# Linear attention and an MLP on one core: even and odd partition runs, weight loads held back, and transposes moved from TensorE to DMA

## The chip, the cores and the metric

The kernel runs on one core of a Trainium2 chip. The metric is device time in microseconds (us) of one execution. The profile is one profiled execution; its span runs from the first to the last instruction and is about 1.7 us shorter than the time of the same run.

Names: PE is TensorE's matmuls, PEld its weight loads, DVE is VectorE, ACT is ScalarE, POOL is GpSimd, SP is SyncE, whose queue issues most transfers here. k(0) is the k input of batch 0, and so on.

## The reference

There are 8 batches of 8 heads, 576 tokens and 64 values per head. Attention is linear, with features of relu times a cosine and a sine of the token's position; then a token-wise MLP follows.

```python
def phi(x, c, s):
    r = np.maximum(x, 0.0)
    return np.concatenate([r * c, r * s], axis=-1)      # 64 -> 128 features
q_p = phi(q, cos_w, sin_w)
k_p = phi(k, cos_w, sin_w)
kv = np.einsum('bhsf,bhsd->bhfd', k_p, v)
z = np.sum(k_p, axis=2)
num = np.einsum('bhsf,bhfd->bhsd', q_p, kv)
den = np.einsum('bhsf,bhf->bhs', q_p, z)[..., None] + 1e-06
x = num / den                                           # then: tokens x 512
h = x @ w_in                                            # 512 x 2048
g = h * np.cos(h)
out = g @ w_out                                         # 2048 x 512
```

## The kernel before

For each batch the 576 tokens lie as 4 tiles of 128 tokens and a remainder of 64, which two batches share. So one half of the 128 partitions holds five tokens each and the other half four. `half(n)` says which half: 64 consecutive partitions. Every load of k, v or q is two transfers, one to each half.

```python
    def half(n):
        return slice(R * n, R * (n + 1))            # R = 64
    ...
    def load(b, name, after=None):
        ...
        if after is not None:                       # holds the load back until `after` is there
            for hf in range(2):
                nc.gpsimd.tensor_copy(
                    out=m[R * hf:R * hf + 1, 0, 0, 0:1], in_=after)
        s_ = srcs[name][b]
        nc.sync.dma_start(
            out=m[half(n)], in_=s_[:, 0:S5, :].rearrange("h (p t) d -> p h t d", t=NT + 1))
        nc.sync.dma_start(
            out=m[half(1 - n), :, 0:NT, :],
            in_=s_[:, S5:S, :].rearrange("h (p t) d -> p h t d", t=NT))
```

The matmuls of this kernel take q features and x with the contracted dimension on the partitions. TensorE transposes both itself, and ACT copies the result out of PSUM, the memory that its matmuls write (`x_trans` is the same with four matmuls a tile):

```python
    def q_trans(b, t):
        ...
        for h in range(H):
            nc.tensor.matmul(
                QP[:, h, :], lhsT=src[:, h].rearrange("p g d -> p (g d)"),
                rhs=IDENT, is_transpose=True)
        qT = apool.tile([P, H, P], F16, name=f"qT{b}_{t}", tag=f"qT{t}")
        nc.scalar.activation(out=qT, in_=QP, func=AF.Copy)
```

The weights are loaded by POOL's queue in four transfers each, cast from f32 to f16 on the way (the page counts 4.19 MB on that queue for the two matrices, which are 8.39 MB in f32). A one-element copy from a tile that a load fills holds a transfer back, because the transfer overwrites that element: POOL's copy for w_out waits 18.24 us for v(1), until 45.65 us, and its transfer leaves at 46.12. Only the first of four is held:

```python
    for name in ("k", "v", "q"):
        load(0, name)
    ...
    nc.gpsimd.tensor_copy(out=w_in_sb[0:1, 0, 0:1], in_=raw[("v", 0)][0:1, 0, 0, 0:1])
    for g in range(4):
        fs = slice(g * Dff // 4, (g + 1) * Dff // 4)
        nc.gpsimd.dma_start(out=w_in_sb[:, :, fs], in_=wi[:, :, fs])
    for f in attention(0, after=w_in_sb[0:1, 0, Dff // 2:Dff // 2 + 1]):
        f()
    nc.gpsimd.tensor_copy(out=w_out_sb[0:1, 0, 0:1], in_=raw[("v", 1)][0:1, 0, 0, 0:1])
    # ... w_out in four transfers
    for s in range(B + 1):                          # MLP of batch s beside attention of batch s+1
        spread(mlp(s), attention(s + 1) if s + 1 < B else [])
```

A scheduler in the build orders each engine's instructions, so the order on an engine need not be that of the code. The traces show it.

## Time and profile before

| | before |
|---|---|
| median of 3 runs | 353.27 us (353.17 to 353.39) |
| span of the profiled run | 351.6 us |
| PE busy, matmuls | 305.9 us, 2448 |
| first matmul of batch 1's MLP | 74.42 us |
| last matmul ends | 345.8 us |

From the profile's page of the kernel before, parts 1 and 2. The rows of part 2 cut the span into 40 slices; a digit is the busy share in tenths.

```profile
PE 305.9 (87%) x2448; PEld 170.8 (49%) x2448; DVE 202.8 (58%) x491; ACT 185.4 (53%) x284; POOL 13.3 (4%) x30
...
PE   0034477799999999999999999999999999999993
...
DMA  7999999829998578940993168202021020220232
```

There are two regimes. From slice 9 to the last but one TensorE is always busy. Before it, TensorE idles much of the time and the DMA row stands mostly at 9. The view of busy time by stretch, asked for the second regime, with the columns named in its header:

```profile
core 0: us, PE busy (x) PEld busy (x) DVE busy (x) ACT busy (x) POOL busy (x), PEclk, DMA share, GB/s
74.42:345.80 271.38, 270.13 (x2109) 148.47 (x2107) 164.54 (x388) 150.19 (x233) 0.00 (x0) 1.00 0.46 99
```

TensorE is idle for 1.25 us of 271.38, at full clock (1.00). Here a matmul removed is time removed. The list of TensorE's waits, longest first (tile, source line, releaser: total, times, longest), lies almost wholly in the first regime:

```profile
PE KV_0_136 L129 <- DVE V_0_75 L118: 17.3, 1, 17.3
PE XP_0_304 L183 <- DVE x_0_254 L174: 5.5, 1, 5.5
PE QP_0_184 L142 <- ACT qp_111 L98: 5.5, 1, 5.5
PE M_362 L237 <- DMA w_in_sb<-in_moe_w_in_dram: 3.0, 1, 3.0
PE QP_0_462 L142 <- DVE qp_352 L100: 2.5, 1, 2.5
PE KV_0_398 L129 <- DVE V_1_76 L118: 1.8, 1, 1.8
```

Why the inputs come late is on POOL's timeline (start, duration, instruction):

```profile
6.44 2.36 POOL L334 DMA_DIRECT2D w_in_sb<-in_moe_w_in_dram  x3
...
45.65 0.18 POOL L337 CAST w_out_sb<-vm_131 1x1 f16<-1x1 f32 x1 [18.24 <-DMA vm_131<-in_v_dram]
```

Weight transfers that nothing holds back leave from 6.44 us and share the DMA engines with k, v and q of batch 0. v(1), which the last line waits for, lands at 45.65 us.

What a transpose costs is on TensorE's timeline between back-to-back matmuls:

```profile
102.64 0.81 PE L237 MATMUL M_1134<-xT_354,w_in_sb 128*128 128x512 f16 x3
103.28 0.39 PE L183 MATMUL XP_1_1142<-IDENT,x_1_1062 128*128 128x128 f16 x4
103.51 1.06 PE L249 MATMUL M_1149<-xTr_717,w_in_sb 128*128 128x128 f16 x16
```

Durations overlap in the pipeline (102.64 + 0.81 is past 103.28), so the cost is start to start: the four x transposes hold TensorE from 103.28 to 103.51, about 0.225 us. Eight q transposes hold it 0.445 us by the same reading (120.83 to 121.27 for one group).

### The profile page before, as it was taken

How to read it: one execution, taken by the hardware profiler on the slowest of the kernel's cores; microseconds unless marked ns; L12 is line 12 of the kernel's file. 1: busy time of each engine (PE TensorE's matmuls, PEld its weight loads, DVE VectorE, ACT ScalarE, POOL GpSimd, SP SyncE). 2: the span in 40 equal slices, each digit the busy share in tenths (PEclk: the TensorE clock that was granted, in tenths of full speed). 3: DMA queues.
4: the chain of work that ended last, by engine and by line, in shares of the span. 5: the costliest groups of instructions: out<-in, count | busy, mean ns of one | idle time of the engine just before them, and what ended most of it. 6: DMA issues, size and time to landing. Idle time of an engine off the chain costs nothing.

```text
span 351.6 us, 6070 instructions
## 1 busy us (share of the span) xinstructions
PE 305.9 (87%) x2448; PEld 170.8 (49%) x2448; DVE 202.8 (58%) x491; ACT 185.4 (53%) x284; POOL 13.3 (4%) x30
## 2 busy tenths in 40 slices
PE   0034477799999999999999999999999999999993
PEld 0034235445565555445574554455655554446441
DVE  0421849989996669438784887445943471444100
ACT  1335437665755575356764665557555753555210
POOL 9120010000000000000000000000000000000000
PEclk9998589989999999999999999999999999999999
DMA  7999999829998578940993168202021020220232
GB/s 152 224 235 248 250 200 237 149 58 209 202 203 170 135 163 158 204 122 10 238 196 85 34 132 184 72 2 62 1 47 44 2 62 0 60 49 13 68 83 60
DMA packets 33083, 42.37 MB, mean 121 GB/s; under 512 B 1824, under 2 KB 30496, under 8 KB 33056
## 3 DMA queue, kind: packets, MB, share of 16 engines
q1 hardware_dynamic: 28544, 37.75, 50.3%
q0 software_dynamic: 4224, 4.19, 7.1%
q8 instruction: 19, 0.31, 0.4%
q10 hardware_dynamic: 288, 0.04, 0.1%
q14 instruction: 8, 0.07, 0.1%
HBM read 36.74 MB, written 9.44 MB: 131 GB/s over the span
## 4 chain that ended last, share of the span: by engine, by line
PE 79%; DMA 5%; issue 5%; DVE 4%; ACT 2%; POOL 1%; POOLq 0%
DMA w_in_sb<-in_moe_w_in_dram 5%; ACT ch L229 1%; PE M_4128 L261 1%; PE M_4109 L261 1%; PE M_4049 L261 1%; PE M_2824 L261 1%; PE M_2741 L261 1%; PE M_2601 L261 1%; PE M_2250 L261 1%; PE M_1948 L261 1%; PE M_1815 L261 1%; PE M_1732 L261 1%; PE M_1592 L261 1%; PE M_1454 L261 1%; PE M_1241 L261 1%
## 5 line engine op out<-in xcount | busy, mean ns | idle before, releaser
L237 PEld LDWEIGHTS <-w_in_sb 128*128 128x128 f16 x512 | 47.2, 99 | 48.6 <-issue 7.6
L129 PE MATMUL KV_0_136<-V_0_75,kp_110 128*128 128x65 f16 x16 | 1.2, 243 | 17.3 <-DVE V_0_75 L118 17.3
L249 PEld LDWEIGHTS <-w_in_sb 128*128 128x128 f16 x256 | 14.8, 98 | 0.2
L129 PEld LDWEIGHTS <-kp_110 128*128 128x128 f16 x32 | 2.2, 131 | 17.3 <-issue 17.3
L261 PEld LDWEIGHTS <-g_3761 128*128 128x128 f16 x64 | 6.2, 97 | 7.6
L261 PEld LDWEIGHTS <-g_3287 128*128 128x128 f16 x64 | 6.2, 98 | 7.3
L261 PEld LDWEIGHTS <-g_751 128*128 128x128 f16 x64 | 6.2, 98 | 7.1
L261 PEld LDWEIGHTS <-g_1760 128*128 128x128 f16 x64 | 6.2, 98 | 7.1
L261 PEld LDWEIGHTS <-g_2769 128*128 128x128 f16 x64 | 6.2, 98 | 7.1
L261 PEld LDWEIGHTS <-g_2278 128*128 128x128 f16 x64 | 6.1, 98 | 7.1
L261 PEld LDWEIGHTS <-g_1269 128*128 128x128 f16 x64 | 6.1, 98 | 7.1
L261 PEld LDWEIGHTS <-g_361 128*128 128x128 f16 x64 | 6.1, 98 | 7.1
L142 PEld LDWEIGHTS <-qp_111 128*128 128x128 f16 x32 | 3.3, 148 | 5.6 <-ACT qp_111 L98 5.6
L142 PE MATMUL QP_0_184<-IDENT,qp_111 128*128 128x128 f16 x8 | 1.0, 311 | 5.5 <-ACT qp_111 L98 5.5
L183 PE MATMUL XP_0_304<-IDENT,x_0_254 128*128 128x128 f16 x4 | 0.7, 301 | 5.5 <-DVE x_0_254 L174 5.5
L100 DVE TENSOR_SCALAR KPR_78<-km_124,CS 64x512 f16<-64x512 f32 x2 | 0.9, 487 | 7.8 <-DMA km_124<-in_k_dram 7.8
L98 ACT ACT_TABLE_LOAD x1 | 1.3, 1283 | 7.2 <-DMA km_83<-in_k_dram 7.2
L100 DVE TENSOR_SCALAR qp_1753<-qm_1483,CS 128x512 f16<-128x512 f32 x8 | 3.7, 461 | 1.9 <-PE QP_3_1486 L142 1.9
L230 DVE TENSOR_TENSOR g_3761<-M_3762,ch 128x512 f16<-128x512 f32 x1 | 0.7, 692 | 6.9 <-ACT ch L229 6.9
L237 PE MATMUL M_362<-xT_113,w_in_sb 128*128 128x512 f16 x4 | 1.9, 622 | 3.0 <-DMA w_in_sb<-in_moe_w_in_dram 3.0
L100 DVE TENSOR_SCALAR qp_2762<-qm_2492,CS 128x512 f16<-128x512 f32 x8 | 3.7, 461 | 1.3 <-PE QP_3_2495 L142 1.3
L98 ACT ACTIVATE qp_111<-qm_89,CS 128x512 f16<-128x512 f32 x4 | 2.6, 711 | 3.1 <-DMA qm_89<-in_q_dram 3.1
(1128 smaller groups left out, 864.6 us busy)
## 6 DMA issues: line engine op xcount, KB each, us to landing
out_dram<-ost SPq DMA_DIRECT2D x32, 256.0 KB, 3.2
w_in_sb<-in_moe_w_in_dram POOLq DMA_DIRECT2D x4, 512.0 KB, 16.8
w_out_sb<-in_moe_w_out_dram POOLq DMA_DIRECT2D x4, 512.0 KB, 17.5
out_dram<-ostr SPq DMA_DIRECT2D x8, 128.0 KB, 2.3
km_83<-in_k_dram SPq DMA_DIRECT2D x1, 640.0 KB, 6.4
vm_86<-in_v_dram SPq DMA_DIRECT2D x1, 640.0 KB, 10.7
qm_89<-in_q_dram SPq DMA_DIRECT2D x1, 640.0 KB, 16.6
km_124<-in_k_dram SPq DMA_DIRECT2D x1, 640.0 KB, 10.5
```

What stands on the lines that cost most here:

```text
L98: nc.scalar.activation(out=out[:, :, g, :], in_=in_, func=AF.Relu, scale=sc)
L100: nc.vector.tensor_scalar(out=out[:, :, g, :], in0=in_, scalar1=0.0, scalar2=sc, op0=ALU.max, op1=ALU.mult)
L129: nc.tensor.matmul(KV[:, hh, :], lhsT=kp[:, t, h].rearrange("p g d -> p (g d)"), rhs=V1[b % 2][:, t, h, :], start=(t == 0), stop=False)
L142: nc.tensor.matmul(QP[:, h, :], lhsT=src[:, h].rearrange("p g d -> p (g d)"), rhs=IDENT, is_transpose=True)
L183: nc.tensor.matmul(XP[:, c, :], lhsT=x2[:, c * P:(c + 1) * P], rhs=IDENT, is_transpose=True)
L229: nc.scalar.activation(out=ch[:, 0:n], in_=M1, func=AF.Sin, bias=PIH, scale=1.0)
L230: nc.vector.tensor_tensor(out=dst, in0=M1, in1=ch[:, 0:n], op=ALU.mult)
L237: nc.tensor.matmul(M1, lhsT=w_in_sb[:, c, j * P:(j + 1) * P], rhs=xts[b][:, c, :], start=(c == 0), stop=(c == NCT - 1))
L249: nc.tensor.matmul(M1[:, jj, :], lhsT=w_in_sb[:, c, j * P:(j + 1) * P], rhs=xts[("r", pr)][:, c, :], start=(c == 0), stop=(c == NCT - 1))
L261: nc.tensor.matmul(M2, lhsT=gts[key][:, j, gsl], rhs=w_out_sb[:, j, :], start=(j == 0), stop=(j == NJT - 1))
```

## The change

It has three intents. The two runs of partitions become the even and the odd ones, so that each load and store spreads over the whole range of partitions. All four transfers of w_in wait for the first of q(0)'s two transfers, all four of w_out for v(1), and q is loaded before v. From batch 2 on, q features and x are transposed by DMA from and to the on-chip memory, not by TensorE and ACT. Beside these, the remainder becomes a fifth tile, padded with zeros, and V is cast in one instruction of five tiles. The core of the diff, cuts marked:

```diff
+    NPE = 2
-    def half(n):
-        return slice(R * n, R * (n + 1))
+    def blocks(ap, n):
+        return ap.rearrange("(p f) ... -> f p ...", f=2)[n]
 ...
-        nc.sync.dma_start(
-            out=m[half(n)], in_=s_[:, 0:S5, :].rearrange("h (p t) d -> p h t d", t=NT + 1))
-        nc.sync.dma_start(
-            out=m[half(1 - n), :, 0:NT, :],
-            in_=s_[:, S5:S, :].rearrange("h (p t) d -> p h t d", t=NT))
 ...
+        nc.sync.dma_start(out=blocks(m, n), in_=five)
+        nc.sync.dma_start(out=blocks(m, 1 - n)[:, :, 0:NT, :], in_=four)
 ...
     def prep_v(b):
 ...
-        nc.vector.tensor_copy(
-            out=V1[b % 2][:, :, :, 0:D],
-            in_=m[:, :, 0:NT, :].rearrange("p h t d -> p t h d"))
-        nc.vector.tensor_copy(out=V1R[b % 2][hf, :, 0:D], in_=m[hf, :, NT, :])
+        vt = raw["v"].rearrange("p h t d -> p t h d")
+        for n, (t0, t1) in enumerate(((0, 2), (2, NT + 1)) if b == 0 else ((0, NT + 1),)):
+            dst = V1[b % 2][:, t0:t1, :, 0:D]
+            if b == 0 and n == 0:
+                nc.scalar.activation(out=dst, in_=vt[:, t0:t1], func=AF.Copy)
+            else:
+                nc.vector.tensor_copy(out=dst, in_=vt[:, t0:t1])
 ...
+    def q_trans_dma(b):
+        qT = apool.tile([P, NT + 1, H, P], F16, name=f"qT{b}", tag="qTd")
+        nc.sync.dma_start_transpose(
+            out=qT.rearrange("f t h p -> f (t h) p"),
+            in_=qps[b].rearrange("p t h g d -> p (t h g d)"))
 ...
     def x_trans(b, t):
 ...
+        if b >= NPE:
+            nc.sync.dma_start_transpose(out=dst, in_=x2)
+            return
 ...
-        steps = [pk(t) for t in range(NT + 1)] + [ld("k"), pv, ld("v")]
-        steps += [of(kv_group, 0), pq(0), of(kv_group, 1), pq(1)]
-        for t in range(2, NT + 1):
-            steps += [of(q_trans, t - 2), pq(t)]
-        steps += [ld("q"), of(q_trans, NT - 1), of(num, 0), of(q_trans, NT),
+        if b == 0:
+            steps = [pk(t) for t in range(NT + 1)] + [ld("k"), pq(0)]
+            for t in range(1, NT + 1):
+                steps += [of(q_trans, t - 1), pq(t)]
+            steps += [ld("q"), of(q_trans, NT), pv, ld("v"), of(kv_group, 0),
+                      of(kv_group, 1), of(num, 0)]
+        elif b >= NPE:
+            steps = [pq(t) for t in range(NT + 1)]
+            steps += [ld("q"), lambda: q_trans_dma(b)]
+            steps += [pk(t) for t in range(NT + 1)]
+            steps += [ld("k"), pv, ld("v"), of(kv_group, 0), of(kv_group, 1), of(num, 0)]
+        else:
+            # ... as before
 ...
-    for name in ("k", "v", "q"):
+    for name in ("k", "q", "v"):
 ...
-    nc.gpsimd.tensor_copy(out=w_in_sb[0:1, 0, 0:1], in_=raw[("v", 0)][0:1, 0, 0, 0:1])
+    nc.gpsimd.tensor_copy(
+        out=w_in_sb[0:1, 0, :].rearrange("p (g f) -> p g f", g=G)[:, :, 0],
+        in_=raw["q"][0:1, 0, 0, 0:1].broadcast_to((1, G)))
 ...
-    nc.gpsimd.tensor_copy(out=w_out_sb[0:1, 0, 0:1], in_=raw[("v", 1)][0:1, 0, 0, 0:1])
+    nc.gpsimd.tensor_copy(
+        out=w_out_sb[0:1, :, 0].rearrange("p (g j) -> p g j", g=G)[:, :, 0],
+        in_=raw["v"][0:1, 0, 0, 0:1].broadcast_to((1, G)))
```

More of the change, by code (lines that the diff above doesn't have):

```diff
@@ L51 @@
             w = fn(theta)
-            cs_np[half(n), n, g, :] = w[:S5].reshape(R, NT + 1)
-            cs_np[half(1 - n), n, g, :NT] = w[S5:].reshape(R, NT)
+            cs_np[n::2, n, g, :] = w[:S5].reshape(R, NT + 1)
+            cs_np[1 - n::2, n, g, :NT] = w[S5:].reshape(R, NT)
     cs_dr = nc.inline_tensor(cs_np, name="cs_const")
@@ L57 @@
     cpool = ctx.enter_context(tc.tile_pool(name="cpool", bufs=1))
-    rpool = ctx.enter_context(tc.tile_pool(name="rpool", bufs=1))
     apool = ctx.enter_context(tc.tile_pool(name="apool", bufs=2))
@@ L68, with tokens @@
     w_out_sb = cpool.tile([P, NJT, Dm], F16, name="w_out_sb")
-    V1 = [cpool.tile([P, NT, H, D1], F16, name=f"V1_{n}") for n in range(2)]
-    KPR = [cpool.tile([P, H, 2, D], F16, name=f"KPR{n}") for n in range(2)]
-    V1R = [cpool.tile([P, H, D1], F16, name=f"V1R{n}") for n in range(2)]
-    QPR = [cpool.tile([P, H, 2, D], F16, name=f"QPR{n}") for n in range(2)]
+    V1 = [cpool.tile([P, NT + 1, H, D1], F16, name=f"V1_{n}") for n in range(2)]
     srcs = {"k": k, "v": v, "q": q}
-    raw, kvzs, kps, qps, qts, xts, gts = {}, {}, {}, {}, {}, {}, {}
+    raw = {nm: cpool.tile([P, H, NT + 1, D], F32, name=f"{nm}m") for nm in srcs}
+    kvzs, kps, qps, qts, xts, gts = {}, {}, {}, {}, {}, {}
+    def tokens(ap, n):
+        return (ap[..., 0:S5, :].rearrange("h (p t) d -> p h t d", t=NT + 1),
+                ap[..., S5:S, :].rearrange("h (p t) d -> p h t d", t=NT))
     def load(b, name, after=None):
@@ L79, in load @@
             return
-        m = rpool.tile([P, H, NT + 1, D], F32, name=f"{name}m{b}", tag=f"{name}m")
-        n = b % 2
+        m, n = raw[name], b % 2
         if after is not None:
-            for hf in range(2):
-                nc.gpsimd.tensor_copy(
-                    out=m[R * hf:R * hf + 1, 0, 0, 0:1], in_=after)
-        s_ = srcs[name][b]
-        nc.sync.dma_start(
-            out=m[half(n)], in_=s_[:, 0:S5, :].rearrange("h (p t) d -> p h t d", t=NT + 1))
-        nc.sync.dma_start(
-            out=m[half(1 - n), :, 0:NT, :],
-            in_=s_[:, S5:S, :].rearrange("h (p t) d -> p h t d", t=NT))
@@ L92, in load, with prep @@
-        raw[(name, b)] = m
-    def feat(b, out, in_, rows, t):
+            nc.gpsimd.tensor_copy(out=m[0:2, 0, 0, 0:1], in_=after)
+        five, four = tokens(srcs[name][b], n)
+        nc.sync.dma_start(out=blocks(m, n), in_=five)
+        nc.sync.dma_start(out=blocks(m, 1 - n)[:, :, 0:NT, :], in_=four)
+    def prep(b, name, dst, t):
+        in_ = raw[name][:, :, t, :]
         for g in range(2):
-            sc = CS[rows, b % 2, g, t:t + 1]
+            sc = CS[:, b % 2, g, t:t + 1]
             if b == 0 and g == 1:
-                nc.scalar.activation(out=out[:, :, g, :], in_=in_, func=AF.Relu, scale=sc)
+                nc.scalar.activation(out=dst[:, t, :, g, :], in_=in_, func=AF.Relu, scale=sc)
@@ L99, in feat @@
             else:
                 nc.vector.tensor_scalar(
-                    out=out[:, :, g, :], in0=in_, scalar1=0.0, scalar2=sc,
+                    out=dst[:, t, :, g, :], in0=in_, scalar1=0.0, scalar2=sc,
                     op0=ALU.max, op1=ALU.mult)
-    ALLP = slice(0, P)
-    def prep(b, name, dst, rem, t):
-        m = raw[(name, b)]
-        if t < NT:
-            feat(b, dst[:, t], m[:, :, t, :], ALLP, t)
-        else:
-            hf = half(b % 2)
-            feat(b, rem[b % 2][hf], m[hf, :, t, :], hf, t)
@@ L115, in prep_v @@
-    def prep_v(b):
-        m = raw[("v", b)]
-        hf = half(b % 2)
-        nc.vector.tensor_copy(
-            out=V1[b % 2][:, :, :, 0:D],
-            in_=m[:, :, 0:NT, :].rearrange("p h t d -> p t h d"))
-        nc.vector.tensor_copy(out=V1R[b % 2][hf, :, 0:D], in_=m[hf, :, NT, :])
+    def prep_v(b):
+        vt = raw["v"].rearrange("p h t d -> p t h d")
[5 more added lines that the diff above has]
+                nc.vector.tensor_copy(out=dst, in_=vt[:, t0:t1])
@@ L127, in kv_group @@
             h = hb * HB + hh
-            for t in range(NT):
+            for t in range(NT + 1):
                 nc.tensor.matmul(
                     KV[:, hh, :], lhsT=kp[:, t, h].rearrange("p g d -> p (g d)"),
-                    rhs=V1[b % 2][:, t, h, :], start=(t == 0), stop=False)
-            nc.tensor.matmul(
-                KV[:, hh, :], lhsT=KPR[b % 2][:, h].rearrange("p g d -> p (g d)"),
-                rhs=V1R[b % 2][:, h, :], start=False, stop=True)
+                    rhs=V1[b % 2][:, t, h, :], start=(t == 0), stop=(t == NT))
         nc.scalar.activation(
             out=kvz[:, hb * HB:(hb + 1) * HB, :], in_=KV, func=AF.Copy)
+    def q_trans_dma(b):
[3 more added lines that the diff above has]
+            in_=qps[b].rearrange("p t h g d -> p (t h g d)"))
+        for t in range(NT + 1):
+            qts[(b, t)] = qT[:, t]
     def q_trans(b, t):
-        src = qps[b][:, t] if t < NT else QPR[b % 2]
+        src = qps[b][:, t]
         QP = ppool.tile([P, H, P], F16, name=f"QP{b}_{t}", tag="ps")
@@ L144, in q_trans @@
                 rhs=IDENT, is_transpose=True)
-        qT = apool.tile([P, H, P], F16, name=f"qT{b}_{t}", tag=f"qT{t}")
+        if t == 0:
+            qTs[b] = apool.tile([P, NT + 1, H, P], F16, name=f"qT{b}", tag="qTd")
+        qT = qTs[b][:, t]
         nc.scalar.activation(out=qT, in_=QP, func=AF.Copy)
         qts[(b, t)] = qT
-    x16s = {}
+    x16s, qTs = {}, {}
     def num(b, t):
@@ L180, in x_trans @@
         x2 = x16s.pop((b, t)).rearrange("p h d -> p (h d)")
+        if t < NT:
+            dst = xts[b][:, :, t * P:(t + 1) * P]
+        else:
+            dst = xts[("r", b // 2)] = apool.tile(
+                [P, NCT, P], F16, name=f"xTr{b}", tag="xTr")
+        if b >= NPE:
+            nc.sync.dma_start_transpose(out=dst, in_=x2)
+            return
         XP = ppool.tile([P, NCT, P], F16, name=f"XP{b}_{t}", tag="ps")
@@ L185, in x_trans @@
                 is_transpose=True)
-        if t < NT:
-            dst = xts[b][:, :, t * P:(t + 1) * P]
-        else:
-            dst = xts[("r", b // 2)] = apool.tile(
-                [P, NCT, P], F16, name=f"xTr{b}", tag="xTr")
         nc.scalar.activation(out=dst, in_=XP, func=AF.Copy)
     def attention(b, after=None):
-        kps[b] = apool.tile([P, NT, H, 2, D], F16, name=f"kp{b}", tag="kp", bufs=1)
-        qps[b] = apool.tile([P, NT, H, 2, D], F16, name=f"qp{b}", tag="qp", bufs=1)
+        kps[b] = apool.tile([P, NT + 1, H, 2, D], F16, name=f"kp{b}", tag="kp", bufs=1)
+        qps[b] = apool.tile([P, NT + 1, H, 2, D], F16, name=f"qp{b}", tag="qp", bufs=1)
         kvzs[b] = apool.tile([P, H, D1], F16, name=f"kvz{b}", tag="kvz", bufs=3)
@@ L200, in pk @@
         def pk(t):
-            return lambda: prep(b, "k", kps[b], KPR, t)
+            return lambda: prep(b, "k", kps[b], t)
         def pq(t):
-            return lambda: prep(b, "q", qps[b], QPR, t)
+            return lambda: prep(b, "q", qps[b], t)
         def ld(name):
@@ L213, in pv @@
             prep_v(b)
-        steps = [pk(t) for t in range(NT + 1)] + [ld("k"), pv, ld("v")]
-        steps += [of(kv_group, 0), pq(0), of(kv_group, 1), pq(1)]
-        for t in range(2, NT + 1):
-            steps += [of(q_trans, t - 2), pq(t)]
-        steps += [ld("q"), of(q_trans, NT - 1), of(num, 0), of(q_trans, NT),
+        if b == 0:
[9 more added lines that the diff above has]
+            steps += [ld("k"), pv, ld("v"), of(kv_group, 0), of(kv_group, 1), of(num, 0)]
+        else:
+            steps = [pk(t) for t in range(NT + 1)] + [ld("k"), pv, ld("v")]
+            steps += [of(kv_group, 0), pq(0), of(kv_group, 1), pq(1)]
+            for t in range(2, NT + 1):
+                steps += [of(q_trans, t - 2), pq(t)]
+            steps += [ld("q"), of(q_trans, NT - 1), of(num, 0), of(q_trans, NT)]
+        steps += [
                   of(num, 1), of(num, 2), of(x_trans, 0), of(num, 3),
@@ L254, in moe1_rem, with rows @@
              M1.rearrange("p j s -> p (j s)"), SM)
+    ALLP = slice(0, P)
     osts = {}
+    def rows(b):
+        ap = out[b * S:(b + 1) * S, :]
+        return (ap[0:S5].rearrange("(p t) m -> p t m", t=NT + 1),
+                ap[S5:S].rearrange("(p t) m -> p t m", t=NT))
     def moe2(key, t, gsl):
@@ L272, in moe2_main @@
         if t % 2 == 1:
-            n, r0 = b % 2, b * S
-            five = out[r0:r0 + S5, :].rearrange("(p t) m -> p t m", t=NT + 1)
-            four = out[r0 + S5:r0 + S, :].rearrange("(p t) m -> p t m", t=NT)
-            nc.sync.dma_start(out=five[:, t - 1:t + 1, :], in_=ost[half(n)])
-            nc.sync.dma_start(out=four[:, t - 1:t + 1, :], in_=ost[half(1 - n)])
+            n = b % 2
+            five, four = rows(b)
+            nc.sync.dma_start(out=five[:, t - 1:t + 1, :], in_=blocks(ost, n))
+            nc.sync.dma_start(out=four[:, t - 1:t + 1, :], in_=blocks(ost, 1 - n))
     def moe2_rem(pr):
@@ L283, in moe2_rem @@
         for n in range(2):
-            r0 = (2 * pr + n) * S
-            five = out[r0:r0 + S5, :].rearrange("(p t) m -> p t m", t=NT + 1)
-            nc.sync.dma_start(out=five[:, NT, :], in_=ost[half(n)])
+            five, _ = rows(2 * pr + n)
+            nc.sync.dma_start(out=five[:, NT, :], in_=blocks(ost, n))
     def mlp(s):
@@ L314, in spread @@
             f()
-    for name in ("k", "v", "q"):
+    for name in ("k", "q", "v"):
+        nc.vector.memset(raw[name][:, :, NT, :], 0.0)
         load(0, name)
@@ L321 @@
     for n in range(2):
-        oth = half(1 - n)
-        nc.gpsimd.memset(KPR[n][oth], 0.0)
         nc.gpsimd.memset(V1[n][:, :, :, D], 1.0)
-        nc.gpsimd.memset(V1R[n][oth], 0.0)
-        nc.gpsimd.memset(V1R[n][half(n), :, D], 1.0)
-        nc.gpsimd.memset(QPR[n][oth], 0.0)
     wi = moe_w_in.rearrange("(c p) f -> p c f", p=P)
     wo = moe_w_out.rearrange("(j p) m -> p j m", p=P)
-    nc.gpsimd.tensor_copy(out=w_in_sb[0:1, 0, 0:1], in_=raw[("v", 0)][0:1, 0, 0, 0:1])
-    for g in range(4):
-        fs = slice(g * Dff // 4, (g + 1) * Dff // 4)
+    G = 4
+    nc.gpsimd.tensor_copy(
+        out=w_in_sb[0:1, 0, :].rearrange("p (g f) -> p g f", g=G)[:, :, 0],
+        in_=raw["q"][0:1, 0, 0, 0:1].broadcast_to((1, G)))
+    for g in range(G):
+        fs = slice(g * Dff // G, (g + 1) * Dff // G)
         nc.gpsimd.dma_start(out=w_in_sb[:, :, fs], in_=wi[:, :, fs])
-    for f in attention(0, after=w_in_sb[0:1, 0, Dff // 2:Dff // 2 + 1]):
+    for f in attention(0, after=w_in_sb[0:2, 0, Dff // 2:Dff // 2 + 1]):
         f()
-    nc.gpsimd.tensor_copy(out=w_out_sb[0:1, 0, 0:1], in_=raw[("v", 1)][0:1, 0, 0, 0:1])
-    for g in range(4):
-        js = slice(g * NJT // 4, (g + 1) * NJT // 4)
+    nc.gpsimd.tensor_copy(
+        out=w_out_sb[0:1, :, 0].rearrange("p (g j) -> p g j", g=G)[:, :, 0],
+        in_=raw["v"][0:1, 0, 0, 0:1].broadcast_to((1, G)))
+    for g in range(G):
+        js = slice(g * NJT // G, (g + 1) * NJT // G)
         nc.gpsimd.dma_start(out=w_out_sb[:, js, :], in_=wo[:, js, :])
```

## The prediction

> **What bounds it now.** Two regimes. By the windows view, from 74.4 us (the timeline's first matmul of batch 1's MLP) to the last matmul's end at 345.8 us TensorE is busy 270 of 271 us at full clock; DVE 61%, ACT 55%. The tail is 5.8 us. The first 74.4 us are start-up: TensorE is busy 36 us, the DMA engines are full to 65 us. POOL's timeline shows why: only one transfer of each weight matrix is held back; three of w_in and three of w_out are issued at 6.4 to 10.3 us, against k, v, q of batch 0. So q lands at 24.4 us, v of batch 1 at 45.6, and TensorE waits 17.3 us for V, 5.5 for q features, 5.5 for x, 3.0 for w_in (the waits).
>
> **Transposes.** In TensorE's timeline eight q transposes hold it 0.445 us, four x transposes 0.225 us. Batches 2 to 7 lose 30 of the first and 27 of the second: 13.4 + 6.1 = 19.4 us, all where TensorE is the chain. About 46 us of ACT copies go too, off the chain. In come six DMA transposes of 1.3 MB and 27 of 128 KB, 11.4 MB together; DMA is busy 46% after 74 us. [...]For q about 15 us of TensorE work or more lie between the last feature and its first use, enough. For x of batches 2, 4 and 6 only 8 us lie between the last numerator and the next stage's first matmul; DVE takes 2 to 3 us[...]. I expect 0 to 2 us of new wait at each of these three boundaries, little at the others.
>
> **Start-up.** All of w_in now waits for q of batch 0, all of w_out for v of batch 1; q goes before v. The partition runs matter too: each load wrote 64 consecutive partitions. [...]The trace fits: a lone k load (200.5 to 209.2 us) moves 1.18 MB in 8.7 us, landing included, below the 235 to 256 GB/s of the mixed start-up. I estimate q at 11 us, x of batch 0 at 26 (40.4 before), v of batch 1 at 40 to 43, because the bytes are unchanged. Batch 1's q features now precede its V copy on DVE, which removes a 2.5 us wait; but batch 2's k features stand among batch 1's gates, a wait of a few us. Batch 1's MLP begins at about 65 us instead of 74.4 (58 to 72).
>
> **Sum.** 65 + (271.4 - 19.4) + 5.8 + about 3 of new waits = 326 us of span; runs read 1.7 above it: 327.5. Range 318 to 338.
>
> **What would show it.** 348 matmuls fewer; no weight load issued before q has landed; k, q, v of batch 0 landed by 15 us; batch 1's MLP from 65 us, from there to the last matmul 255 us; TensorE's waits on DMA-written xT under 2 us per boundary; ACT busy near 140 us.
>
> **What would make it wrong.** DMA transposes far slower than copies, or holding the SP queue so that loads, stores and x come late: several us at each of six boundaries. Or half-partition writes were not the limit and start-up stays byte-bound near 72.

Cut passages are marked: two sentences and a clause on how fast DMA transposes are and on the reach of a load, which no trace had shown. The sum came to 326 us of span, 327.5 us of time. The stage times of the start-up (the 65 us of the sum among them) and the 0 to 2 us of wait for x stand as estimates. Measured, the 27 transposes of x landed 2.4 to 4.9 us after their issue.

## The result, and the profile after

| | before | after |
|---|---|---|
| median | 353.22 us (4 runs) | 327.77 us (327.18 to 329.17, 4 runs) |
| ratio of fast runs | | 0.9289 (95%: 0.9256 to 0.9322) |
| span of the profiled run | 351.6 | 327.4 |
| first matmul of batch 1's MLP | 74.42 | 67.45 |
| last matmul ends | 345.8 | 322.45 |

A ratio is the mean time of one kernel's fast runs over the mean of the other's fast runs in the same rounds, so it is not quite the ratio of the two medians. The profiled one after the change is the slowest of its four (329.17 us). The median is 25.4 us lower, and 0.3 us from the predicted 327.5.

The page of the changed kernel, the totals and the DMA row:

```profile
PE 287.3 (88%) x2100; PEld 152.7 (47%) x2100; DVE 211.2 (65%) x486; ACT 148.9 (45%) x228; POOL 8.3 (3%) x19
...
DMA  7999699519669947986599739949510241010221
```

Its stretch from batch 1's MLP to the last matmul, with the columns of the stretch shown before:

```profile
67.45:322.45 255.00, 251.84 (x1761) 129.93 (x1759) 167.31 (x376) 113.28 (x177) 0.00 (x0) 1.00 0.57 145
```

There are 348 matmuls fewer in the kernel, all in this stretch (2109 to 1761). The stretch is 16.4 us shorter, the start-up 7.0, the tail 0.85 (4.95 after 5.8). TensorE's idle time in the stretch grew from 1.25 to 3.16 us. The changed kernel was profiled once more as a0 (below): its stretch took 255.0 us too, but batch 1's MLP began at 65.51 us. So the stretch repeats, and the start-up moves by 2 us between two executions of one kernel. TensorE's list of waits shows where it idles:

```profile
PE QP_0_115 L137 <- ACT qp_97 L97: 12.9, 1, 12.9
PE KV_0_371 L118 <- DVE V_1_73 L110: 8.8, 1, 8.8
PE XP_3_316 L188 <- DVE x_3_301 L171: 3.5, 1, 3.5
...
PE M_2694 L250 <- DVE x_0_2639 L171: 0.8, 1, 0.8
...
PE NUM_0_1_2625 L159 <- ACT kvz_2413 L121: 0.3, 1, 0.3
```

No wait on a DMA is among them. The last line shown stands for six like it, one in each of batches 2 to 7, about 2 us together. In the kernel before, q transposes stood between the kv matmuls and the first numerators; now nothing covers ACT's copy of kvz.

POOL's timeline now:

```profile
8.91 0.41 POOL L345 CAST w_in_sb<-qm 1x4 f16<-1x4 f32 x1 [7.72 <-DMA qm<-in_q_dram]
9.63 1.62 POOL L350 DMA_DIRECT2D w_in_sb<-in_moe_w_in_dram  x2 [0.31 <-POOL w_in_sb L345]
...
36.75 0.19 POOL L353 CAST w_out_sb<-vm 1x4 f16<-1x4 f32 x1 [15.01 <-DMA vm<-in_v_dram]
```

The first transfer of q(0) has landed at 8.91 us, no weight leaves earlier, and v(1) has landed at 36.75 us (45.65 before). The second transfer of q(0) is what DVE's features wait for, in the changed kernel and then in the kernel before:

```profile
10.39 2.60 DVE L99 TENSOR_SCALAR qp_97<-qm,CS 128x512 f16<-128x512 f32 x4 [0.72 <-DMA qm<-in_q_dram]
```

```profile
24.39 1.88 DVE L100 TENSOR_SCALAR qp_111<-qm_89,CS 128x512 f16<-128x512 f32 x4 [3.65 <-DMA qm_89<-in_q_dram]
```

So the whole of q(0) is there at 10.39 us, where it was there at 24.39. The bytes did not shrink. What changed is their order and the rate, in the stretch view of the first loads, before and then after (the last number is GB/s; the one before it is the DMA share, which can read a little over 1):

```profile
5.00:10.00 5.00, 0.00 (x0) 0.00 (x0) 0.78 (x2) 2.30 (x3) 4.92 (x8) 1.00 1.13 208
```

```profile
5.00:10.00 5.00, 0.00 (x0) 0.00 (x0) 2.46 (x6) 2.82 (x4) 0.78 (x2) 1.00 1.07 361
```

One thing got worse. DVE's timeline of the changed kernel around the arrival of v(1):

```profile
37.14 4.60 DVE L99 TENSOR_SCALAR qp_328<-qm,CS 128x512 f16<-128x512 f32 x10
41.67 2.81 DVE L110 CAST V_1_73<-vm 128x2560 f16<-128x2560 f32 x1
```

and that of the kernel before:

```profile
48.26 1.22 DVE L118 CAST V_1_76<-vm_131 128x2048 f16<-128x2048 f32 x1
```

v(1) is there at 36.75 us, but DVE first computes ten q features, and then casts V for 2.81 us. The cast of 4/5 of the elements took 1.22 us before (and 0.43 for the remainder). TensorE's 8.8 us wait is for this.

### The profile page after: what moved, and what is told of

It is laid out like the page before. It is cut to its first block, busy times and chain, and to the rows that moved or that the text cites. A ratio compares the mean times of both kernels' runs of the same rounds, so it can differ in the third digit from the quotient of the medians.

```text
span 327.4 us, 5404 instructions
## 1 busy us (share of the span) xinstructions
PE 287.3 (88%) x2100; PEld 152.7 (47%) x2100; DVE 211.2 (65%) x486; ACT 148.9 (45%) x228; POOL 8.3 (3%) x19
## 4 chain that ended last, share of the span: by engine, by line
PE 77%; ACT 8%; DVE 7%; DMA 4%; issue 2%; POOL 0%; ACTq 0%; DVEq 0%
DMA km<-in_k_dram 4%; ACT ch L242 2%; DVE qp_328 L99 1%; DVE V_1_73 L110 1%; ACT qT_444 L143 1%; ACT qT_124 L143 1%; PE M_2289 L280 1%; PE M_1439 L280 1%; PE M_3622 L280 1%; PE M_3583 L280 1%; PE M_3523 L280 1%; PE M_3415 L280 1%; PE M_3355 L280 1%; PE M_3296 L280 1%; PE M_3235 L280 1%
## 5 line engine op out<-in xcount | busy, mean ns | idle before, releaser
L250 PEld LDWEIGHTS <-w_in_sb 128*128 128x128 f16 x512 | 48.2, 99 | 53.3 <-issue 4.3
L262 PEld LDWEIGHTS <-w_in_sb 128*128 128x128 f16 x256 | 14.6, 98 | 0.9
L137 PE MATMUL QP_0_115<-IDENT,qp_97 128*128 128x128 f16 x8 | 1.0, 311 | 12.9 <-ACT qp_97 L97 12.9
L110 DVE CAST V_1_73<-vm 128x2560 f16<-128x2560 f32 x4 | 11.2, 2811 | 0.0
L110 DVE CAST V_0_72<-vm 128x2560 f16<-128x2560 f32 (+1 forms) x4 | 10.2, 2550 | 0.8 <-DMA vm<-in_v_dram 0.8
L137 PEld LDWEIGHTS <-qp_97 128*128 128x128 f16 x40 | 4.2, 149 | 12.9 <-ACT qp_97 L97 12.9
L280 PEld LDWEIGHTS <-g_3255 128*128 128x128 f16 x64 | 6.3, 98 | 7.5
L280 PEld LDWEIGHTS <-g_1569 128*128 128x128 f16 x64 | 6.3, 98 | 7.5 <-issue 0.2
L280 PEld LDWEIGHTS <-g_719 128*128 128x128 f16 x64 | 6.3, 98 | 7.5 <-issue 0.2
L280 PEld LDWEIGHTS <-g_2010 128*128 128x128 f16 x64 | 6.2, 98 | 7.3
L280 PEld LDWEIGHTS <-g_337 128*128 128x128 f16 x64 | 6.2, 98 | 7.3
L280 PEld LDWEIGHTS <-g_2860 128*128 128x128 f16 x64 | 6.2, 98 | 7.3
L280 PEld LDWEIGHTS <-g_1160 128*128 128x128 f16 x64 | 6.2, 98 | 7.3
L280 PEld LDWEIGHTS <-g_2419 128*128 128x128 f16 x64 | 6.2, 98 | 7.3
L99 DVE TENSOR_SCALAR qp_2853<-qm,CS 128x512 f16<-128x512 f32 x10 | 4.3, 479 | 4.6 <-DMA qT_2468<-qp_2412 4.6
L118 PEld LDWEIGHTS <-kp_327 128*128 128x128 f16 x40 | 2.5, 133 | 9.7 <-issue 9.6
L99 DVE TENSOR_SCALAR kp_327<-km,CS 128x512 f16<-128x512 f32 x10 | 4.2, 481 | 3.2 <-DMA km<-in_k_dram 3.2
L99 DVE TENSOR_SCALAR qp_2412<-qm,CS 128x512 f16<-128x512 f32 x10 | 4.2, 481 | 2.5 <-DMA qT_2051<-qp_2003 2.5
L99 DVE TENSOR_SCALAR qp_2003<-qm,CS 128x512 f16<-128x512 f32 x10 | 4.1, 482 | 1.9 <-DMA qT_1618<-qp_1562 1.9
L99 DVE TENSOR_SCALAR qp_1153<-qm,CS 128x512 f16<-128x512 f32 x10 | 4.5, 471 | 1.4 <-DMA qT_768<-qp_712 1.4
```

Of the source, the lines that this page charges most:

```text
L99: nc.vector.tensor_scalar(out=dst[:, t, :, g, :], in0=in_, scalar1=0.0, scalar2=sc, op0=ALU.max, op1=ALU.mult)
L110: nc.vector.tensor_copy(out=dst, in_=vt[:, t0:t1])
L118: nc.tensor.matmul(KV[:, hh, :], lhsT=kp[:, t, h].rearrange("p g d -> p (g d)"), rhs=V1[b % 2][:, t, h, :], start=(t == 0), stop=(t == NT))
L137: nc.tensor.matmul(QP[:, h, :], lhsT=src[:, h].rearrange("p g d -> p (g d)"), rhs=IDENT, is_transpose=True)
L250: nc.tensor.matmul(M1, lhsT=w_in_sb[:, c, j * P:(j + 1) * P], rhs=xts[b][:, c, :], start=(c == 0), stop=(c == NCT - 1))
L262: nc.tensor.matmul(M1[:, jj, :], lhsT=w_in_sb[:, c, j * P:(j + 1) * P], rhs=xts[("r", pr)][:, c, :], start=(c == 0), stop=(c == NCT - 1))
```

## The experiments

The kernels were run with the kernel before beside them: e1 to e4; e5, e9, e8 and c1; and the last four rows. All give the reference's results. A run is called slow when it is more than 1.5% above the fastest of the same kernel; the ratios use fast runs alone, while the medians count slow runs too (e1, e5 and c1 have some). "Step" below is the difference of two ratios times 353.2 us: against the changed kernel's 0.9289, or, for the last four rows, against the ratio of the changed kernel run again, 0.9281. From the intervals of the two ratios, a step is uncertain by about 1.4 to 2.5 us either way.

| run | what is different from the changed kernel | median us | ratio (95%) | step us |
|---|---|---|---|---|
| e1_te_transposes | all transposes on TensorE | 348.21 | 0.9849 (0.981 to 0.9887) | +19.8 |
| e2_half_runs | 64 consecutive partitions | 338.72 | 0.9597 (0.9565 to 0.963) | +10.9 |
| e3_weights_free | only one transfer of four held | 337.85 | 0.9558 (0.9524 to 0.9592) | +9.5 |
| e9_half_and_free | both of these | 338.98 | 0.9589 (0.9541 to 0.9636) | +10.6 |
| e8_before_held | the kernel before, all transfers held | 352.44 | 0.9974 (0.9919 to 1.0028) | -0.9 against before |
| e4_v_cast_by_head | V cast, head outermost | 326.43 | 0.9235 (0.9202 to 0.9268) | -1.9 |
| e5_v_before_q | v(1) loaded before q(1) | 328.44 | 0.9282 (0.9234 to 0.933) | -0.2 |
| c1_cast_kvq | the last two | 326.41 | 0.9149 (0.9086 to 0.9212) | -4.9 (fast runs) |
| a0_changed_again | nothing | 327.77 | 0.9281 (0.9252 to 0.931) | 0 |
| e6_double_q_transpose | each q transpose twice | 335.85 | 0.9506 (0.9478 to 0.9534) | +7.9 |
| e7_dma_from_1 | DMA transposes from batch 1 | 337.6 | 0.9557 (0.953 to 0.9584) | +9.7 |
| c2_cast_gap | e4, and other work before the numerators | 322.78 | 0.9134 (0.9107 to 0.916) | -5.2 |

### e1_te_transposes: the transposes back on TensorE

```diff
-    NPE = 2
+    NPE = 8
```

> The changed kernel with the limit NPE raised from 2 to 8: all transposes back on TensorE, everything else (partition runs, held-back weights, order of the first loads) kept. Theory: the DMA transposes are free and the 57 TensorE groups cost their full 19.4 us, less about 2 us of small waits on kvz that the changed kernel has and this one should not have: about +17 us, 345 us. The start-up stays, batch 1's MLP begins at 67 to 68 us. Rival: DMA transposes compete with loads and cost something; then undoing them costs less, +8 to +13 us, 336 to 341 us.

Three fast runs gave 346.92 to 348.38 us, by the ratios 19.8 us over the changed kernel. So about 20 of the 25.4 us hang on the transposes. That is a little over what the theory expected, and well over the rival's. Undoing should also take back the new waits, so that 16.4 us was to be expected from the trace's own bookkeeping. The remaining 3.4 us could not be traced: the profiled execution was a slow one, 668.84 us at a recorded clock of 1.00, in which 512-column matmuls took 677 ns on the mean (379 in groups of the kernel before). It is left out of every comparison, so where e1's time went is not shown by a trace.

### e2_half_runs and e3_weights_free: the two halves of the start-up

e2 goes back to consecutive partitions and keeps the rest:

```diff
-        return ap.rearrange("(p f) ... -> f p ...", f=2)[n]
+        return ap[R * n:R * (n + 1)]
 ... # the cosine table and the held element follow suit
```

> The changed kernel with each load and store over 64 consecutive partitions again, all else kept. Theory: [...]the 361 GB/s of 5 to 10 us falls to about 200 to 220 GB/s, q of batch 0 lands at 13 to 15 us instead of 10.4, v of batch 1 at 41 to 45 us instead of 36.8, batch 1's MLP begins 4 to 7 us later: 332 to 335 us. Rival: the partition runs do nothing, the faster loads of the start come from the weights being out of the way: within 1 us of 327.8, 340 GB/s or more at 5 to 10 us.

(200 to 220 GB/s is the estimate. The kernel before read 208 in that window.)

e3 keeps even and odd, and holds one transfer of four back, of w_out likewise:

```diff
-        out=w_in_sb[0:1, 0, :].rearrange("p (g f) -> p g f", g=G)[:, :, 0],
-        in_=raw["q"][0:1, 0, 0, 0:1].broadcast_to((1, G)))
+        out=w_in_sb[0:1, 0, 0:1], in_=raw["q"][0:1, 0, 0, 0:1])
```

> The changed kernel with only the first transfer of each weight matrix held back, as in the kernel before; all else kept. Theory: three transfers each of w_in and w_out then go first, q of batch 0 lands at 17 to 22 us instead of 10.4 and x of batch 0 is ready near 40 us instead of 31; batch 1's MLP begins 3 to 6 us later: 331 to 334 us. Rival: the start is bound by the sum of the bytes up to v of batch 1, which the order does not change, and x of batch 0 has slack: v of batch 1 lands near 37 us as before and the time stays within 1 us of 327.8.

Each cost about 10 us, more than expected, and together more than the whole start-up gain. The traces put the cost in the start-up: batch 1's MLP begins at 76.57 us in e2 and at 74.48 in e3 (67.45 and 65.51 in the two traces of the changed kernel), and the stretch after it takes 255.9 and 255.0 us (255.0 in both). The stretch view of the first loads, for e2 and then for e3:

```profile
5.00:10.00 5.00, 0.00 (x0) 0.00 (x0) 0.37 (x1) 0.41 (x1) 0.00 (x0) 1.00 1.13 202
```

```profile
5.00:10.00 5.00, 0.00 (x0) 0.00 (x0) 0.00 (x0) 0.00 (x0) 0.87 (x2) 1.00 1.15 254
```

With consecutive halves the loads run at 202 GB/s where they ran at 361; in e2 every 5-us window to 50 us reads 201 to 206. That the partition runs set the rate is shown by e2; why they do is not shown. e3 is another matter: its DMA engines are as full (1.15), but the weights take their share, and the first transfer of q(0), landed at 8.91 us in the changed kernel, lands at 15.17. e3 is also a little harsher than the kernel before: POOL has less to clear first, so the free weights leave from 1.28 us, where they left from 6.44. The same holds for e9 below.

e2 and e3 are also late for different reasons. In e2 v(1) lands at 49.27 us and DVE casts it at once. In e3 it lands at 44.03, and DVE's timeline reads:

```profile
44.51 4.17 DVE L99 TENSOR_SCALAR qp<-qm,CS 128x512 f16<-128x512 f32 x10
48.60 2.81 DVE L110 CAST V<-vm 128x2560 f16<-128x2560 f32 x1
```

So in e3 a V that has landed waits 4.6 us behind the ten q features.

### e9_half_and_free and e8_before_held: do the two halves add up?

e9 is e2 and e3 together. e8 is the kernel before with all four transfers of each weight held (of w_out likewise, for v(1)):

```diff
-    nc.gpsimd.tensor_copy(out=w_in_sb[0:1, 0, 0:1], in_=raw[("v", 0)][0:1, 0, 0, 0:1])
+    nc.gpsimd.tensor_copy(
+        out=w_in_sb[0:1, 0, :].rearrange("p (g f) -> p g f", g=4)[:, :, 0],
+        in_=raw[("v", 0)][0:1, 0, 0, 0:1].broadcast_to((1, 4)))
```

> The changed kernel with both start-up parts undone: 64 consecutive partitions and only the first transfer of each weight held back; DMA transposes, first-load order and cast kept. Alone, the two undone parts cost 10.9 and 10.1 us. Theory: both delay the same landing of batch 1's v, so together they cost less than the sum, 12 to 17 us: 340 to 345 us; then the rest of the change (q before v, the slower cast) costs 7 to 12 us against the 332.9 us that the kernel before would reach with the 20.4 us of the transposes alone. Rival: they add up, 348 to 350 us.

> The kernel before with all four transfers of each weight matrix held back, nothing else changed. Theory: k, v and q of batch 0 land by 18 us instead of 24[...]; v of batch 1 lands at 41 to 43 instead of 45.6 us: 4 to 6 us faster, 347 to 349 us. Rival: [...]holding back gives nothing without the partition runs: within 1 us of 353.3.

(In the second, two clauses on the rate and its reason are cut; e8's 5-us windows from 5 to 50 us read 197 to 206 GB/s. The first counts by medians: 10.1 and 20.4 us where the ratios give 9.5 and 19.8.)

Both theories for e9 fell: it cost 10.6 us, the same as either part alone, and not more. The rival for e8 was right in its number: holding the weights alone is worth nothing that can be seen, at 0.9974 with 1 inside the interval. Its v(1) lands 2.2 us earlier (43.43 us), yet batch 1's MLP begins at 74.36 us (74.42 before). The two parts are not two gains. Either one pays only where the other is there too:

| | consecutive halves | even and odd |
|---|---|---|
| weights free (changed kernel otherwise) | 0.9589 (e9), v(1) at 49.38 | 0.9558 (e3), v(1) at 44.03 |
| weights held (changed kernel otherwise) | 0.9597 (e2), v(1) at 49.27 | 0.9289, v(1) at 36.75 |

The arrival of v(1) in the second part of each cell follows the time, but for e3: its v(1) lands 5.3 us before that of e9 and its time is not apart from e9's, since V then stands behind the q features. An account that fits the rates, though no run tests it further: with consecutive halves the loads run at about 204 GB/s (e2), and letting weights flow beside them brings the whole to 249 to 258 GB/s up to 35 us (e9); so holding the weights loses as much as it wins. With even and odd partitions the loads alone ran at 361 GB/s, and then who goes first matters.

By the ratios e9 is 14.5 us faster than the kernel before, and it has neither half of the start-up change. The transposes were measured at 19.8 us. The remaining 5.3 us is a loss that belongs to the rest of the change: by the traces, q in front of V on DVE, the slower cast, the new waits on kvz and, in e9 alone, weights that leave earlier than in the kernel before. That split is argued, not measured; e4 and c2 below measure parts of it.

### e4_v_cast_by_head: the cast's outermost dimension

```diff
-        vt = raw["v"].rearrange("p h t d -> p t h d")
 ...
-            dst = V1[b % 2][:, t0:t1, :, 0:D]
+            dst = V1[b % 2][:, t0:t1, :, 0:D].rearrange("p t h d -> p h t d")
+            vt = raw["v"][:, :, t0:t1, :]
 ... # both casts then read vt as it is
```

The elements are the same; the instruction walks 8 heads of 5 tiles where it walked 5 tiles of 8 heads. In the traces the cast of 5 tiles took 2.81 us (2560 elements a partition) and that of 4 tiles 1.22 us (2048). Why is not shown; what the run tests is whether an 8 in front, in place of the 5, brings the speed back.

> The changed kernel with V's cast walked head by head (8 outermost in source and destination) instead of run by run (5 outermost in the source), same elements. Theory: [...]by head it takes 1.4 to 1.5 us instead of 2.81, batch 1's first KV matmul moves from 44.5 to 43.1 us and the 0.8 us wait for x of batch 6 goes: 1.5 to 2.2 us faster, about 326 us. Rival: the cast is slow for another reason (DMA traffic into SBUF at the time, or the wider rows): it stays at 2.8 us and the time at 327.8.

The line of this cast in the changed kernel (odd batches), and then in e4 (all batches); the three numbers are the least, the median and the greatest ns:

```profile
L110 DVE CAST V_1_73<-vm x4: 2808/2810/2814, 41.7 to 222.5; 128x2560 f16<-128x2560 f32 x4
```

```profile
L110 DVE CAST V<-vm x8: 964/1484/1489, 14.4 to 220.9; 128x2560 f16<-128x2560 f32 x7, 128x1536 f16<-128x1536 f32 x1
```

2.81 us became 1.48, and the 0.8 us wait of `M_2694` is gone. In the changed kernel DVE cast V of batch 7 from 222.46 to 225.27 us, just ahead of x of batch 6 (226.55 to 227.30 us), whose end `M_2694` waits for. The first kv matmul of batch 1 came at 42.22 us instead of 44.53; but in a0's trace of the unaltered kernel it came at 42.50, so a gain in the start-up is not shown. The stretch from batch 1's MLP on is 254.0 us, 1.0 shorter than in both traces of the changed kernel. The time is 1.9 us lower by ratio, as expected, and 1.3 by median, with intervals that overlap.

### e5_v_before_q and c1_cast_kvq: v(1) ahead of q(1)

```diff
-            steps += [ld("q"), of(q_trans, NT), pv, ld("v"), of(kv_group, 0),
+            steps += [of(q_trans, NT), pv, ld("v"), ld("q"), of(kv_group, 0),
```

> The changed kernel with batch 1's v loaded before its q (batch 0 keeps q first). Theory: the changed kernel's longest start-up wait, 8.8 us for batch 1's V, is made by its own order: v lands last (36.8 us) and its cast stands behind ten q features on DVE. With v first it lands near 33 us, the first KV matmul of batch 1 moves from 44.5 to about 40 us, and part of that reaches the end: 323 to 325 us. Rival: DVE has the same work to do before batch 1's x is ready, so only the order of waits changes: within 1.5 us of 327.8.

No gain: 0.9282 against 0.9289, though the wait that it aimed at was TensorE's second largest. Its profiled execution was again slow (1700.16 us, left out), so the reason was looked for in c1, which has the edits of e4 and e5:

> The changed kernel with the by-head cast and batch 1's v before q. Theory: both act on the same wait for batch 1's V and on different parts of it (landing and order; the cast's own 1.4 us), so they add: 321 to 323.5 us. Rival: after v is moved, the start is bound by DVE's total work or by x of batch 0, and the cast adds less than 0.7 us to the other.

c1's profile is of a fast run. v(1) lands at 32.76 us and the kv matmuls begin at 36.46, 8 us earlier than in the changed kernel, so the aim is met. TensorE's list of waits shows what took its place:

```profile
PE KV L118 <- DVE V L110: 3.0, 1, 3.0
...
PE QP L137 <- DVE qp L99: 2.3, 1, 2.3
PE M L250 <- DMA xT<-x: 2.0, 1, 2.0
```

The wait for V falls from 8.8 to 3.0 us, and q features are now waited for, and in batch 6 a transposed x. c1 has two modes: 323.30 to 323.87 us in three runs and 328.95 to 329.98 in three others, which are classed as slow. Only the first three are in its ratio; the mean of all six would make the step 1.7 us in place of 4.9, so c1's gain holds for one of its modes only. In the profiled fast run batch 1's MLP begins at 61.16 us, and the stretch after it is 1.1 us longer (256.1), by the wait for the transposed x. What sets the mode stays open; nothing but a lower mean clock (0.957 to 0.963 against 0.974 to 0.989) was seen. In a0 the clock did not order the times, against what was expected of that run: 328.73 and 328.77 us at 0.973, 327.25 and 327.49 at 0.960.

### e6_double_q_transpose: how much slack has the q transpose?

```diff
     def q_trans_dma(b):
+        scrap = cpool.tile([P, (NT + 1) * H, P], F16, name=f"scrap{b}", tag="scrap")
+        nc.sync.dma_start_transpose(
+            out=scrap, in_=qps[b].rearrange("p t h g d -> p (t h g d)"))
```

Each q transpose is issued a second time, to a tile that nobody reads. The prediction had said that q has "about 15 us of TensorE work or more" in hand.

> The changed kernel with every DMA transpose of q issued twice (the second into a tile that nothing reads), 7.9 MB more through the DMA engines and 6 to 8 us more of the SP queue per batch. Theory: q has 15 us or more of slack and nothing on the critical chain stands behind it on the SP queue, so the time stays within 1.5 us of the changed kernel beside it. Rival: the transposes are near the chain (queue, rings, or the next batch's features that wait for the transpose to have read): 3 us or more slower, waits of TensorE on xT or on qT in the trace.

It cost 7.9 us, as the rival had it. The longest new wait of TensorE, and then one of DVE:

```profile
PE M L253 <- DVE g L246: 3.9, 1, 3.9
```

```profile
DVE qp L99 <- DMA scrap<-qp: 12.9, 3, 9.6
```

TensorE never waits for a DMA transpose, of q or of x, which the rival had named. It waits for a gate product g of the MLP (3.9 us here, 1.7 in an earlier batch). DVE stands at the next batch's first q feature until 228.86 us, and makes the g that is waited for only after it, at 229.26 us: that feature overwrites the single buffer of q features, which the transposes still read. The stretch from batch 1's MLP on is 7.2 us longer (262.2). So the slack of a DMA transpose is not only the time to the first use of its result, but also the time until its source is overwritten. In the changed kernel the same wait is there (DVE waits for q transposes for 4.6, 2.5, 1.9 and 1.4 us in four batches) and costs TensorE nothing.

### e7_dma_from_1: DMA transposes one batch earlier

```diff
-    NPE = 2
+    NPE = 1
```

> The changed kernel with NPE = 1: batch 1 uses DMA transposes too. Ten TensorE groups less (3.4 us), but they lie in the start-up, where TensorE is not the bound. Theory: q of batch 1 must then be loaded, made into features and transposed by DMA (8 to 10 us to landing) before the first numerator, and x waits for a DMA transpose before the first MLP matmul, so batch 1's MLP begins later: 2 to 6 us slower than the changed kernel beside it. Rival: the start-up is bound by DVE and ACT, ACT loses 8 us of copies: up to 3 us faster.

The direction was right, the size of 9.7 us larger than expected. TensorE's new wait:

```profile
PE NUM L159 <- DMA qT<-qp: 8.8, 1, 8.8
```

In batch 1 the transpose's time is exposed: TensorE has little else to do there. Batch 1's MLP begins at 70.30 us, 2.9 to 4.8 us late. That is not all: the stretch after it is 5.9 us longer (260.9). TensorE waits for DVE and ACT between 80 and 97 us for about 4 us, and the 16 matmuls from 97.69 us take 4.71 us, where others of their kind take 3.62; the runs' mean clocks are 0.940 to 0.958 (0.960 to 0.976 in a0). DVE's q features wait for q transposes for 14.7 us in five waits, up to 8.5 us, as in e6. So a start at batch 2 is better than at batch 1; a later one was not tried.

### c2_cast_gap: the parts that help, together

c2 has e4's cast, and moves one step so that a group of MLP matmuls falls between the kv matmuls and the first numerators:

```diff
-            steps += [ld("k"), pv, ld("v"), of(kv_group, 0), of(kv_group, 1), of(num, 0)]
+            steps += [ld("k"), pv, of(kv_group, 0), of(kv_group, 1), ld("v"), of(num, 0)]
```

> The by-head cast, and in batches 2 to 7 one MLP group of TensorE between the last KV matmul and the first numerator (the issue of v's next load moves behind the KV groups to make that place). Theory: the six waits of 0.3 us for the copy of kvz, which the removed q transposes used to cover, go: 1.5 to 2 us faster than the by-head cast alone, 3 to 4 us faster than the changed kernel beside it, 324 to 325 us. Rival: they reappear elsewhere (x of batches 2, 4, 6 one slot later): within 1 us of the by-head cast alone.

Six fast runs, 321.48 to 323.83 us: 5.0 us by median, or 1.6%, under the changed kernel in the same rounds, with intervals apart. It has the lowest ratio (c1's fast runs are level with it within the intervals), and the gain is more than was expected. Its timeline of batch 6, where the MLP group now stands between:

```profile
215.78 0.77 PE L118 MATMUL KV<-V,kp 128*128 128x65 f16 x20
216.38 1.02 PE L250 MATMUL M<-xT,w_in_sb 128*128 128x512 f16 x4
217.25 0.42 PE L159 MATMUL NUM<-kvz,qT 128*128 128x65 f16 x8
```

The waits on kvz are down to one of 0.3 us, in the start-up. That is about 2 us of the gain over e4; the two are 3.6 us apart (0.9235 and 0.9134). They were run at other times. By the traces the stretch from batch 1's MLP on is 251.3 us, where e4's is 254.0 and the changed kernel's 255.0; the start-up, 63.6 us after 65.9 in e4, has the same program for batches 0 and 1, so its part of the difference may be scatter.

## Why the prediction was right

**The transposes: right.** The term was 19.4 us, 348 matmuls fewer. The traces show 348 fewer and a stretch of 255.0 us (predicted 255), 16.4 us shorter: TensorE's busy time there fell by 18.3 us and its idle time grew by 1.9 (about 2 us of waits on kvz and 0.8 on x came, 1.2 of older waits on x went). e1 puts the transposes back for 19.8 us; the 3.4 us between the two stay open.

**The new waits: right in size, wrong in place.** The prediction had "about 3 of new waits" on x written by DMA, at the boundaries before batches 2, 4 and 6. There is none on DMA. There are waits on kvz, which the removed q transposes had covered, and one on x whose releaser is DVE, behind a slow cast; c2 and e4 remove each. So this term came out right because one error replaced another, and that is luck. So, in part, is the total's 0.3 us: the two traces of the changed kernel alone differ by 2.0 us.

**The start-up: right in cause and roughly in size.** Batch 1's MLP begins at 67.45 us (65.51 in a0), where 65 was predicted (58 to 72). e2, e3, e8 and e9 show that the partition runs and the held-back weights are the cause, with a correction: the prediction told them as two contributions, and the runs show one, which needs both. The stages inside it were off, in both directions: v(1) landed at 36.75 us rather than at 40 to 43, and x of batch 0 was ready at 31 rather than at 26. The first MLP matmul (`M_338`, 31.07 us) waits for ACT's copy of x, after the chain of features, q, V cast and x; the 3.5 us before it is x held up on DVE behind the k features of batch 1, whose load had not landed. The prediction had named that collision as "a wait of a few us", but for batch 2's k features among batch 1's gates.

**One step failed.** "Batch 1's q features now precede its V copy on DVE, which removes a 2.5 us wait." They do precede it, and the 2.5 us wait is gone, but they put 4.6 us of features and then a cast of 2.81 us in front of the kv matmuls, which wait 8.8 us for V where they waited 1.8. What of it reached the end is not measured: e5, with v(1) first, gains nothing (its trace is a slow one), and c1's trace shows a shorter wait for V and other waits instead. That the cast would go from 1.22 + 0.43 us to 2.81 us was not foreseen at all; the diff shows one instruction in place of two, and not that a 5 has become the outermost count (with 8 outermost the cast took 1.48 us, e4).

**The rate of the transposes.** A q transpose moves 1.31 MB and landed 7.9 to 10.3 us after its issue. The stretch view of two windows of the changed kernel in which one runs nearly alone:

```profile
167.00:171.00 4.00, 4.00 (x20) 1.76 (x19) 4.00 (x4) 0.97 (x2) 0.00 (x0) 1.00 1.17 218
201.00:205.00 4.00, 4.00 (x21) 1.80 (x19) 1.89 (x1) 0.87 (x2) 0.00 (x0) 1.00 1.16 217
```

That is 217 to 218 GB/s, against 361 for the first loads of the same kernel: lower by two fifths, and hidden all the same.

ACT is busy 148.9 us, not "near 140"; in the stretch it is busy 113.28 of 255.00 us.

## What to carry to other kernels

Before removing work from the busiest engine, list what that work covered: six copies of kvz became waits the moment the q transposes left, and one moved step took them back. Profile one kernel twice before a shift of 2 us in its start-up is given a cause: here two traces of the same kernel differ by that much. Two changes to the start-up may be one: the order of the loads paid only when the loads ran at the higher rate (361 GB/s against 201 to 206), and the rate only when the order was right, so undo each and both before giving either a number. For work moved to DMA, count the slack on both sides, to the first use of the result and to the next write of the source.

## What else was measured

- How long a transpose occupies the queue that issues it: SP's timeline of the changed kernel shows 6.13 to 8.16 us for the six q transposes of 1.31 MB, and mostly 1.2 us for one of 128 KB, against 0.6 to 0.7 us for most loads.
- Two whole executions (668.84 us of e1 and 1700.16 us of e5) ran slow at a recorded clock of 1.00. 512-column matmuls took 677 ns on the mean in the first; in the second, 12 from 47.31 us took 15.83 us, where 20 take 4.48 us in a0.
